# A float32 attention item's product with v turned around, its division moved behind that product, and the first weight decoding kept in source order

## The chip, the core and the metric

The program runs on one NeuronCore of a Trainium2 chip, in one launch. Its engines work side by side, each through its own queue of instructions, in order: TensorE (PE; its weight loads are shown as PEld), VectorE (DVE), ScalarE (ACT), GpSimd (POOL), and SyncE (SP), which only issues DMAs. The metric is the device time of one execution in microseconds. The kernel before takes 966.29 us (median of three runs, 964.24 to 967.59).

## The reference

Causal attention with a window of 128 positions and a slope per head, then two MLPs one behind the other, all in float32:

```python
scores = scale * np.matmul(q, k.transpose(0, 1, 3, 2))            # B=4, H=8, S=576, D=64
scores = np.where(mask, scores + bias[None], -1000000000.0)       # mask: 0 <= rel < 128
attn = np.exp(scores - np.max(scores, axis=-1, keepdims=True))
attn = attn / (np.sum(attn, axis=-1, keepdims=True) + 1e-09)
x = np.matmul(attn, v).transpose(0, 2, 1, 3).reshape(2304, 512)
h = x @ w_in                                                      # 512 -> 2048
x = (np.maximum(h, 0.0) + alpha * np.minimum(h, 0.0)) @ w_out     # 2048 -> 512
h = x @ w_in2
out = (h * (1.0 / (1.0 + np.exp(-1.702 * h)))) @ w_out2
```

The weights arrive as float64.

## The kernel before

**Attention.** An item is one batch, one head and one part of the sequence: part 0 has 256 queries, part 1 has 320. The 64 items come in the order part 0 (batch by batch, head by head), then part 1. The first 16 (`n < FP`) are computed in plain float32, the others by products of high and low halves. For a float32 item, TensorE makes the scores (`a_qk`: tile `s`), VectorE adds the bias and finds the row's extreme value (`a_bias`: tile `tt`, the extreme in `st`), ScalarE takes the exponential and sums it along each row in the same pass (`a_exp`), VectorE turns the sums into reciprocals (`a_recip`), and `a_norm` multiplies each row by its reciprocal: 128 columns on VectorE, 256 on ScalarE. TensorE then transposes the result in three 128x128 pieces (`a_trans`: tile `pt` in PSUM), ScalarE copies them to SBUF (`a_pt_hi`), and `a_av` multiplies: `vz`, padded with zeros to 128 columns so that the two heads of a pair land in the two halves of one PSUM tile `x`, is the stationary operand, and `pt` is streamed, 256 and 128 columns. After the second head of a pair `a_x3` splits `x` into `xh` (ScalarE) and `xl` (VectorE), the input of the first MLP.

**Weights.** Each of the 32 chunks of the first MLP (`w_load`: 512 KB into one of four buffers `ws`) is decoded from float64: two scalings on ScalarE (`w_scale`), then on VectorE `w_sign`, `w_shift` and `w_add`; `w_split` copies the high half `wh` (ScalarE, for two chunks VectorE) and subtracts to get the low half `wl` (VectorE). A buffer is loaded anew after its `w_add`.

**Order.** Rounds `n` = 0 to 9 stand ahead of the first MLP, each with the stages of several items and two decoding steps. Then come the MLP's steps `(k, f)`: `k` is a block of 256 tokens, `f` one of 16 slices of the hidden layer. `m1_h` makes the slice's hidden values (tile `h`, 12 matmuls), `m1_n` and `m1_g` the activation, `m1_o` adds the slice's part of the output (12 matmuls, two steps later). Every two steps carry one more item, and the steps of block 0 carry the rest of the decoding. Slice `f` of block 0 needs chunk `2f` for `m1_h` and chunk `2f + 1` for `m1_o`; block 0 needs items 0 to 7, block 1 items 8 to 15. The program is written in this order, but a scheduler moves instructions on each engine, except where `pin` (`tc.keep_in_program_order`) holds one at its place; before, nothing ahead of the last block of the first MLP is held. The second MLP follows and is not touched.

Of the kernel before, what the change touches and what calls it, by code (L numbers as in the profile page):

```python
# [21 lines left out]
P = 128  # L22
# [43 lines left out]
def tile_window_attention__then__two_mlps(  # L66
# [83 lines left out]
    def w_sign(i):  # L150
        lo, hi = w_words(i)
        pin(nc.vector.tensor_scalar(hi, hi, -0x80000000, None, op0=ALU.bitwise_and))
# [115 lines left out]
    vzs = [apf.tile([P, 2, P], F32, name=f"vz{i}") for i in range(2)]  # L268
# [54 lines left out]
    @stage  # L323
    def a_split_v(n, b, u, h, U):
        nv = (2, 4)[u]
        vr = raw_of(n)[:, UCOLS[u] - nv * D : UCOLS[u]].rearrange("p (j d) -> p j d", d=D)
        if n < FP:
            d0 = (h % 2) * D
            nc.gpsimd.tensor_copy(vzs[n % 2][:, :, d0 : d0 + D], vr)
            return  # L330
        vp = ar["v", n % 2]
        nc.scalar.copy(vp[:, :nv, :D], vr)
        sub("pool", vp[:, :nv, D:], vr, vp[:, :nv, :D])
# [40 lines left out]
    @stage  # L374
    def a_exp(n, b, u, h, U):
        tt, s = tts[n % 2], sts[n % 2]
        for i, (c0, rows, kk, keys) in enumerate(U["chunks"]):
            t = tt[:rows, i * 256 : i * 256 + keys]
            nc.scalar.activation(
                t, t, AF.Exp, bias=s[:rows, i : i + 1], scale=-1.0, accum_out=s[:rows, 4 + i : 5 + i]  # L380
            )

    @stage
    def a_recip(n, b, u, h, U):
        s = sts[n % 2]
        m = len(U["chunks"])
        nc.vector.tensor_scalar(s[:, 8 : 8 + m], s[:, 4 : 4 + m], 1e-9, None, op0=ALU.add)
        nc.vector.reciprocal(s[:, 12 : 12 + m], s[:, 8 : 8 + m])  # L388

    @stage  # L390
    def a_norm(n, b, u, h, U, eng):
        tt, s = tts[n % 2], sts[n % 2]
        for i, (c0, rows, kk, keys) in enumerate(U["chunks"]):
# [34 lines left out]
    def a_av(n, b, u, h, U):  # L428
        if n < FP:
            x = st["x", n] = st["x", n - 1] if h % 2 else ps_a.tile([P, 512], F32, tag="a", name="x")  # L430
            pt, vz = pts[n % 2], vzs[n % 2]
            for j in range(2):
                nc.tensor.matmul(  # L433
                    x[:, j * P : 256], vz[:, j, :], pt[:, j * 256 : 256 + j * P],
                    start=(h % 2 == 0 and j == 0), stop=(h % 2 == 1 and j == 1), skip_group_check=True,
                )
            return
# [12 lines left out]
        st["x", n] = x  # L450

# [17 lines left out]
    def a_x3(n, b, u, h, U):  # L469
# [3 lines left out]
        if n < FP:  # L473
            xp = st["x", n]
# [232 lines left out]
    for t in vzs:  # L707
        nc.gpsimd.memset(t, 0.0)
# [24 lines left out]
    nc.gpsimd.tensor_scalar(beta, alph, -1.0, 1.0, op0=ALU.mult, op1=ALU.add)  # L733
    for n in range(H + 2):

        a_av(n - 2)
# [5 lines left out]
        if n + 1 < H + 2:  # L742
            a_qk(n + 1)
        a_bias(n)
# [3 lines left out]
        a_recip(n - 1)  # L748
        w("shift")
        a_norm(n - 1, "mix")  # L750
        a_trans(n - 1)
        w("add")
        w_ahead()
        w("scale")
        a_x3(n - 2)
        w("split")
        w("sign")
        w("shift")
        a_pt_hi(n - 1, 0)
        a_pt_hi(n - 1, 1)  # L760
        if n + 2 < H + 2:
            a_split(n + 2)
        w("add")
        w_ahead()
        w("scale")
    n = H + 2
    a_split(n)
    for i in range(2):
        a_pt_lo(n - 2, i)
    a_recip(n - 1)  # L770
    a_norm(n - 1, "mix")
    a_av(n - 2)
    a_x1(n - 2)
    a_x2(n - 2)
    a_x3(n - 2)
# [5 lines left out]
    for s, (k, f) in enumerate(steps):  # L781
        n = H + 2 + s // 2
        norm = "mix" if k == 0 else "dve"
        if (k, f) == (KM, 0):
            pinned.append(True)
# [26 lines left out]
        else:  # L812
            a_av(m)
            if n == FP:
# [15 lines left out]
        if k == 0:  # L830
            w("split")
        m1_o(k - (f < LAG), (f - LAG) % NF)
# [131 lines left out]
```

## Time and profile before

| | |
|---|---|
| median of three runs | 966.29 us |
| the profiled execution | 967.92 us |
| its span (first to last instruction) | 966.1 us |
| busy: PE, DVE, ACT, POOL | 97%, 75%, 56%, 9% of the span |
| first instruction on VectorE that computes | 5.38 us |
| `xl` of heads 6 and 7 of batch 0 starts (block 0 can begin in full) | 59.24 us |
| `xl` of heads 6 and 7 of batch 1 starts (block 1 can begin in full) | 125.49 us |

All times in the rows are microseconds from the start of the span. An instruction's duration includes its latency; where two follow each other without a wait, the distance of their starts is the share of the engine's time that one takes.

### The profile page before, as it was taken

How to read it: one execution, taken by the hardware profiler on the slowest of the kernel's cores; microseconds unless marked ns; L12 is line 12 of the kernel's file. 1: busy time of each engine (PE TensorE's matmuls, PEld its weight loads, DVE VectorE, ACT ScalarE, POOL GpSimd, SP SyncE). 2: the span in 40 equal slices, each digit the busy share in tenths (PEclk: the TensorE clock that was granted, in tenths of full speed). 3: DMA queues.
4: the chain of work that ended last, by engine and by line, in shares of the span. 5: the costliest groups of instructions: out<-in, count | busy, mean ns of one | idle time of the engine just before them, and what ended most of it. 6: DMA issues, size and time to landing. Idle time of an engine off the chain costs nothing.

```text
span 966.1 us, 17886 instructions
## 1 busy us (share of the span) xinstructions
PE 939.6 (97%) x6536; PEld 871.2 (90%) x6536; DVE 721.6 (75%) x1789; ACT 536.4 (56%) x1343; POOL 89.8 (9%) x127
## 2 busy tenths in 40 slices
PE   5899999999999999999999999999999999999997
PEld 3579889999999999999988888888898889999997
DVE  6998967767888888887666864697233798878876
ACT  6987766666767667676534443564232644333433
POOL 1000021122222222222000000000000000000000
PEclk9999999999999999999999999999999999999999
DMA  8654521222222223212022335566432333443323
GB/s 266 187 185 148 184 79 56 78 72 66 89 67 88 67 66 89 67 66 89 1 69 81 124 112 182 186 219 200 155 113 88 140 140 114 142 142 113 132 85 109
DMA packets 43895, 112.44 MB, mean 116 GB/s; under 512 B 5024, under 2 KB 15008, under 8 KB 43808
## 3 DMA queue, kind: packets, MB, share of 16 engines
q1 hardware_dynamic: 43808, 111.31, 35.3%
q8 instruction: 51, 0.84, 0.3%
q14 instruction: 36, 0.29, 0.1%
HBM read 82.98 MB, written 28.31 MB: 115 GB/s over the span
## 4 chain that ended last, share of the span: by engine, by line
PE 92%; DMA 3%; ACT 2%; DVE 1%; issue 1%; SPq 0%; DVEq 0%; ACTq 0%
PE h L494 21%; PE h L592 20%; PE p L659 17%; PE o L545 17%; PE p L545 5%; PE x L445 3%; PE pt L412 3%; DMA ws<-in_w_out_dram 2%; PE s L352 1%; PE s L353 1%; PE s L343 1%; PE x L433 1%; ACT ws L148 1%; DMA ws<-in_w_in_dram 0%; ACT oh L102 0%
## 5 line engine op out<-in xcount | busy, mean ns | idle before, releaser
L494 PE MATMUL h<-xh,wh 128*128 128x256 f32 (+1 forms) x512 | 153.7, 302 | 1.0 <-ACT xh L480 0.7
L494 PE MATMUL h<-xh,wl 128*128 128x256 f32 (+1 forms) x512 | 153.6, 300 | 0.0
L494 PE MATMUL h<-xl,wh 128*128 128x256 f32 (+1 forms) x512 | 153.5, 300 | 0.1
L659 PE MATMUL p<-wh,oh 128*128 128x256 f32 x504 | 136.2, 284 | 1.0 <-ACT oh L102 0.6
L659 PE MATMUL p<-wl,oh 128*128 128x256 f32 x504 | 136.1, 283 | 0.0
L545 PE MATMUL o<-gh,wl 128*128 128x256 f32 x448 | 127.5, 286 | 0.0
L545 PE MATMUL o<-gh,wh 128*128 128x256 f32 x448 | 125.4, 286 | 0.0
L545 PE MATMUL o<-gl,wh 128*128 128x256 f32 x448 | 125.2, 281 | 0.0
L659 PE MATMUL p<-wh,ol 128*128 128x256 f32 x504 | 119.2, 284 | 1.0 <-DVE ol L107 1.0
L592 PE MATMUL h<-x2h,wh 128*128 128x512 f32 (+1 forms) x320 | 117.8, 368 | 0.0
L592 PE MATMUL h<-x2l,wh 128*128 128x512 f32 (+1 forms) x320 | 117.7, 368 | 0.0
L592 PE MATMUL h<-x2h,wl 128*128 128x512 f32 (+1 forms) x320 | 117.7, 368 | 0.0
L606 DVE TENSOR_TENSOR g<-h,sg 128x512 f32<-128x512 f32 (+1 forms) x80 | 51.0, 637 | 79.6 <-ACT sg L602 79.5
L602 ACT ACTIVATE sg<-h 128x512 f32<-128x512 f32 (+1 forms) x80 | 44.5, 556 | 107.2 <-PE h L592 106.9
L494 PEld LDWEIGHTS h<-xh,wh 128*128 128x128 f32 x512 | 97.9, 192 | 6.7 <-ACT xh L480 1.9
L494 PEld LDWEIGHTS h<-xl,wh 128*128 128x128 f32 x512 | 98.5, 192 | 5.0 <-DVE st L388 1.3
L494 PEld LDWEIGHTS h<-xh,wl 128*128 128x128 f32 x512 | 98.3, 192 | 2.9
L659 PEld LDWEIGHTS p<-wh,oh 128*128 128x128 f32 x504 | 96.4, 192 | 2.1 <-ACT oh L102 2.0
L659 PEld LDWEIGHTS p<-wl,oh 128*128 128x128 f32 x504 | 96.7, 192 | 0.1
L519 DVE SCALAR_TENSOR_TENSOR g<-n,beta,h 128x256 f32<-128x256 f32 x112 | 53.2, 476 | 46.6 <-ACT n L509 46.4
L659 PEld LDWEIGHTS p<-wh,ol 128*128 128x128 f32 x504 | 86.3, 192 | 1.7 <-DVE ol L107 1.6
L509 ACT ACTIVATE n<-h 128x256 f32<-128x256 f32 x112 | 42.8, 384 | 79.9 <-PE h L494 79.5
(107 smaller groups left out, 2270.7 us busy)
## 6 DMA issues: line engine op xcount, KB each, us to landing
ws<-in_w_in_dram SPq DMA_DIRECT2D x32, 512.0 KB, 3.6
ws<-in_w_out_dram SPq DMA_DIRECT2D x32, 512.0 KB, 3.9
raw<-in_u_dram SPq DMA_DIRECT2D x32, 512.0 KB, 3.4
g2d<-g SPq DMA_DIRECT2D x32, 512.0 KB, 3.4
gr<-g2d SPq DMA_DIRECT2D x32, 512.0 KB, 3.2
raw<-in_u_dram SPq DMA_DIRECT2D x16, 320.0 KB, 2.8
wd<-x2d SPq DMA_DIRECT2D x36, 128.0 KB, 3.0
out_dram<-ob SPq DMA_DIRECT2D x16, 256.0 KB, 3.9
```

The lines of the kernel that those rows point to most:

```text
L148: pin(nc.scalar.mul(lo, lo.bitcast(U32), 2.0**-29))
L343: nc.tensor.matmul(o[:, :keys], raw[:, c0 : c0 + rows], raw[:, 256 + kk : 256 + kk + keys], start=True, stop=True)
L412: nc.tensor.transpose(banks[bank][:, dst : dst + P], src, ident)
L445: nc.tensor.matmul(x[:, oc : oc + nq], v, p[:, col : col + nq], start=(i == 0 and k == 0), stop=(i == len(js) - 1 and k == 1), skip_group_ ...
L494: nc.tensor.matmul(ph, w[:, 0, c * P : (c + 1) * P], x[:, c, r : r + n], start=(c == 0 and i == 0), stop=(c == NC - 1 and i == 2),)
L509: nc.scalar.activation(n, ph, AF.Relu, scale=-1.0)
L519: nc.vector.scalar_tensor_tensor(g, n, beta[:, f : f + 1], ph, op0=ALU.mult, op1=ALU.add)
L545: nc.tensor.matmul(o, w[:, 1, c * P : (c + 1) * P], g, start=(f == 0 and (k == KM or c % 2 == 0) and i == 0), stop=(f == NF - 1 and i == 2 ...
L592: nc.tensor.matmul(ph[:, :n], w[:, f % 2, c * P : (c + 1) * P], x[:, c, :n], start=(c == 0 and i == 0), stop=(c == NC - 1 and i == 2),)
L602: nc.scalar.activation(sg[:, :n], ph[:, :n], AF.Sigmoid, scale=1.702)
L606: nc.vector.tensor_tensor(g[:, f % 2, :n], ph[:, :n], sg[:, :n], op=ALU.mult)
L659: nc.tensor.matmul(o[:, m, :], g[:, a, m * P : (m + 1) * P], w, start=(p == 0 and m == 0 and i == 0), stop=(p == NF // 2 - 1 and i == 2), ...
```

## The change

A float32 item is no longer normalised ahead of its product with v. The exponential is taken without the sum. In `a_av` the transposed exponentials `pt` become the stationary operand, and `vz`, now the 64 columns of v and a column of ones, is streamed: three matmuls of 65 columns, so that the 65th column of the result is the row's sum. The result has queries as rows; for a pair of heads it lies in the PSUM tile `xq`. The new stage `a_div` runs once for a pair: it adds 1e-9 to the four columns of sums, takes reciprocals, and writes the product as an SBUF tile `xq`. `a_x3` then transposes that in two 128x128 pieces into a PSUM tile `x`.

In the rounds ahead of the MLP an item's product now stands in the round of its transposes (it was one round later), the rounds hold 18 decoding steps where they held 20, and all decoding instructions there are held in source order. In the steps of block 0 every fourth step has one decoding step more.

```diff
 def w_sign(i):
     lo, hi = w_words(i)
-        pin(nc.vector.tensor_scalar(hi, hi, -0x80000000, None, op0=ALU.bitwise_and))
+        sign = nc.vector.tensor_scalar(hi, hi, -0x80000000, None, op0=ALU.bitwise_and)
+        if pinned or i < 2 * NF:
+            tc.keep_in_program_order(sign)
...
-    vzs = [apf.tile([P, 2, P], F32, name=f"vz{i}") for i in range(2)]
+    vzs = [apf.tile([P, 2, D + 1], F32, name=f"vz{i}") for i in range(2)]
+    xq = apf.tile([P, 2, 2, D], F32, name="xq")
...
     def a_exp(n, b, u, h, U):
+            if n < FP:
+                nc.scalar.activation(t, t, AF.Exp, bias=s[:rows, i : i + 1], scale=-1.0)
+                continue
...
     def a_av(n, b, u, h, U):
-            for j in range(2):
+            for c, j, col in ((0, 0, 0), (1, 0, 128), (1, 1, 256)):
                 nc.tensor.matmul(
-                    x[:, j * P : 256], vz[:, j, :], pt[:, j * 256 : 256 + j * P],
-                    start=(h % 2 == 0 and j == 0), stop=(h % 2 == 1 and j == 1), skip_group_check=True,
+                    x[:, c, h % 2, :], pt[:, col : col + P], vz[:, j, :],
+                    start=(c == j == h % 2 == 0), stop=(c == j), skip_group_check=True,
                 )
...
+    def a_div(n, b, u, h, U):
+        if n >= FP or h % 2 == 0:
+            return
+        s, x = sts[n % 2], st["xq", n]
+        r, f = (s[:, i : i + 4].rearrange("p (c h) -> p c h", c=2) for i in (8, 12))
+        nc.vector.tensor_scalar(r, x[:, :, :, D], 1e-9, None, op0=ALU.add)
+        nc.vector.reciprocal(f, r)
+        nc.vector.tensor_tensor(xq, x[:, :, :, :D], f.unsqueeze(3).to_broadcast([P, 2, 2, D]), op=ALU.mult)
...
         if n < FP:
-            xp = st["x", n]
+            xp = ps_a.tile([P, 512], F32, tag="a", name="x")
+            for i in range(2):
+                nc.tensor.transpose(xp[:, i * P : (i + 1) * P], xq[:, i, :, :], ident)
...
-        nc.gpsimd.memset(t, 0.0)
+        nc.gpsimd.memset(t, 1.0)
...
+    pinned.append(True)
     for n in range(H + 2):
-        a_av(n - 2)
+        a_trans(n - 1)
         a_split_v(n)
...
+        a_pt_hi(n - 1, 0)
         a_bias(n)
         w("split")
         w("sign")
         a_exp(n)
-        a_recip(n - 1)
+        a_av(n - 1)
         w("shift")
-        a_norm(n - 1, "mix")
-        a_trans(n - 1)
         w("add")
+        a_div(n - 1)
         w_ahead()
         w("scale")
-        a_x3(n - 2)
-        w("split")
-        w("sign")
-        w("shift")
...
+        both = n % 5 < 4
+        if both:
+            w("split")
+            w("sign")
+        a_x3(n - 1)
+        if both:
+            w("shift")
+            w("add")
+            w_ahead()
+            w("scale")
...
+        if (k, f) == (0, 0):
+            pinned.clear()
...
             a_av(m)
+            a_div(m)
...
         if k == 0:
             w("split")
+            if f % 4 == 3:
+                w_decode(lim)
+                w("split")
```

The order of the queues differs only in about the first 1,150 instructions of TensorE, the first 440 of VectorE and the first 325 of ScalarE, which is up to the first steps of block 1; behind that the rows of all engines are the same as before.

VectorE in the rounds ahead of the MLP, around the `xl` of heads 4 and 5 of batch 0 (`wl` are the low halves of weights, `wd` and `ws` a chunk in decoding, `st` the sums and reciprocals), before:

```order
L157 SCALAR_TENSOR_TENSOR wd<-wd,ws 128x512
L107 TENSOR_TENSOR wl_447<-wd,wh_446 128x512
L388 RECIPROCAL st_149<-st_149 128x2
L107 TENSOR_TENSOR xl<-x,xh 128x256
L107 TENSOR_TENSOR wl_488<-wd,wh_487 128x512
L162 ISA wd<-ws,wd 128x1024
L399 TENSOR_SCALAR tt_147<-tt_147,st_149 128x128
L387 TENSOR_SCALAR st_148<-st_148 128x2
L152 TENSOR_SCALAR ws<-ws 128x512
L388 RECIPROCAL st_148<-st_148 128x2
```

In the changed kernel, there around the `xl` of heads 6 and 7 of batch 0:

```order
L107 TENSOR_TENSOR wl_458<-wd,wh_457 128x512
L152 TENSOR_SCALAR ws<-ws 128x512
L465 TENSOR_SCALAR st_149<-xq 128x4
L159 SCALAR_TENSOR_TENSOR wd<-wd,ws 128x512
L466 RECIPROCAL st_149<-st_149 128x4
L164 ISA wd<-ws,wd 128x1024
L467 TENSOR_TENSOR xq<-xq,st_149 128x256
L107 TENSOR_TENSOR wl_502<-wd,wh_501 128x512
L152 TENSOR_SCALAR ws<-ws 128x512
L159 SCALAR_TENSOR_TENSOR wd<-wd,ws 128x512
L107 TENSOR_TENSOR xl<-x,xh 128x256
```

The reciprocals and the multiplication of each item are gone, three instructions for a pair have come, and the same slice of weights (the sixth, with its last low half `wl_447` or `wl_458`) that stood beside the pair 4 and 5 stands beside the pair 6 and 7.

TensorE at the end of block 0, where the product of item 15 (`x` or `xq`) is made, before:

```order
L412 MATMUL pt<-ident,tt_147 128x128
L352 MATMUL s<-kh,q 128x192
L353 MATMUL s<-kl,q 128x192
L352 MATMUL s<-kh,q 128x256
L353 MATMUL s<-kl,q 128x256
L412 MATMUL pt<-ident,tt_147 128x128 x2
L433 MATMUL x<-pt_161,vz_159 128x256
L433 MATMUL x<-pt_161,vz_159 128x128
L494 MATMUL h<-xh,wh_226 128x256
L494 MATMUL h<-xh,wh_270 128x256
```

In the changed kernel (`wh_1197` is a slice of block 0, `o` its output):

```order
L419 MATMUL pt<-ident,tt_147 128x128
L354 MATMUL s<-kh,q 128x192
L355 MATMUL s<-kl,q 128x192
L354 MATMUL s<-kh,q 128x256
L355 MATMUL s<-kl,q 128x256
L419 MATMUL pt<-ident,tt_147 128x128 x2
L513 MATMUL h<-xh,wh_1197 128x256
L513 MATMUL h<-xl,wh_1197 128x256
L440 MATMUL xq<-vz_159,pt_162 128x65 x3
L564 MATMUL o_732<-gh,wh_1080 128x256
L564 MATMUL o_733<-gh,wh_1080 128x256
```

Before, the product stands directly between its transposes and the matmuls that need its `xh` (heads 6 and 7 for slices 0 and 1 of block 1, whose other parts stand ahead of it). In the change 35 matmuls of `h` and `o` stand between the product and the transposes of `xq`, and more behind those, ahead of the first matmul that reads the result.

## Rows read from the trace of the kernel before

**Rows 1.** The page: busy time by engine; PE's busy tenths in 40 slices.

```profile
PE 939.6 (97%) x6536; PEld 871.2 (90%) x6536; DVE 721.6 (75%) x1789; ACT 536.4 (56%) x1343; POOL 89.8 (9%) x127
...
PE   5899999999999999999999999999999999999997
```

**Rows 2.** Stretches: PE, PEld, DVE, ACT, POOL busy (instructions), PEclk, DMA share, GB/s.

```profile
60.00:70.00 10.00, 9.94 (x49) 8.51 (x49) 9.49 (x26) 9.07 (x24) 0.30 (x1) 1.00 0.49 143
...
80.00:100.00 20.00, 20.00 (x164) 19.39 (x163) 18.08 (x46) 15.83 (x37) 0.81 (x2) 1.00 0.53 171
100.00:125.00 25.00, 23.22 (x171) 20.71 (x170) 20.36 (x58) 18.89 (x52) 2.61 (x6) 1.00 0.54 177
125.00:150.00 25.00, 24.35 (x193) 23.95 (x194) 18.46 (x62) 16.80 (x56) 5.70 (x11) 0.93 0.21 68
```

**Rows 3.** Timeline of VectorE: start, length, what; two low halves.

```profile
59.24 0.42 DVE L107 TENSOR_TENSOR xl<-x,xh 128x256 fp32r<-128x256 f32 x1
...
125.49 0.42 DVE L107 TENSOR_TENSOR xl<-x,xh 128x256 fp32r<-128x256 f32 x1
```

**Rows 4.** Timeline of VectorE in the rounds ahead of the MLP, back to back.

```profile
49.30 0.16 DVE L388 RECIPROCAL st<-st 128x2 f32<-128x2 f32 x1
49.38 0.40 DVE L107 TENSOR_TENSOR xl<-x,xh 128x256 fp32r<-128x256 f32 x1
49.70 0.68 DVE L107 TENSOR_TENSOR wl<-wd,wh 128x512 fp32r<-128x512 f32 x1
50.30 0.69 DVE L162 CUSTOM_DVE_ANT_0 wd<-ws,wd 128x1024 uint16<-128x1024 uint16 x1
50.90 0.32 DVE L399 TENSOR_SCALAR tt<-tt,st 128x128 f32<-128x128 f32 x1
...
51.54 0.16 DVE L388 RECIPROCAL st<-st 128x2 f32<-128x2 f32 x1
51.66 0.69 DVE L157 SCALAR_TENSOR_TENSOR wd<-wd,ws 128x512 int32<-128x512 int32 x1
52.27 0.42 DVE L152 TENSOR_SCALAR ws<-ws 128x512 int32<-128x512 int32 x1
52.61 0.28 DVE L399 TENSOR_SCALAR tt<-tt,st 128x128 f32<-128x128 f32 x1
52.80 0.68 DVE L162 CUSTOM_DVE_ANT_0 wd<-ws,wd 128x1024 uint16<-128x1024 uint16 x1
```

**Rows 5.** Groups of ScalarE, 0 to 66 us: busy, mean ns, idle before.

```profile
L397 ACT ACTIVATE tt<-tt,st 128x256 f32<-128x256 f32 x10 | 5.0, 500 | 0.0
...
L379 ACT ACTIVATION_READ_ACCUMULATOR tt<-tt,st 128x1 f32 x20 | 4.0, 198 | 0.0
```

**Rows 6.** Waits, 0 to 66 us: who waited for whom, in total, times, longest.

```profile
DVE ws L152 <- ACT wd L147: 2.1, 3, 1.0
```

**Rows 7.** Timeline of PE at four places: start, length, what, idle before.

```profile
63.75 0.41 PE L494 MATMUL h<-xl,wh 128*128 128x256 f32 x1
63.96 0.41 PE L494 MATMUL h<-xh,wl 128*128 128x256 f32 x1
...
67.83 0.28 PE L494 MATMUL h<-xh,wh 128*128 128x256 f32 x1
67.95 0.28 PE L494 MATMUL h<-xl,wh 128*128 128x256 f32 x1
...
123.88 0.92 PE L433 MATMUL x<-pt,vz 128*128 128x256 f32 x4 [0.88 <-ACT pt L419]
125.51 0.74 PE L494 MATMUL h<-xh,wh 128*128 128x256 f32 x2 [0.71 <-ACT xh L480]
```

**Rows 8.** Chain that ended last, in order of time: start, length, what.

```profile
89.56 0.33 PE pt L412 x3
...
93.42 0.65 PE x L433 x4
```

More of the change, by code (lines that the diff above doesn't have):

```diff
@@ L327, in a_split_v @@
         if n < FP:
-            d0 = (h % 2) * D
-            nc.gpsimd.tensor_copy(vzs[n % 2][:, :, d0 : d0 + D], vr)
+            nc.gpsimd.tensor_copy(vzs[n % 2][:, :, :D], vr)
             return
@@ L386, in a_recip @@
         m = len(U["chunks"])
+        if n < FP:
+            return
         nc.vector.tensor_scalar(s[:, 8 : 8 + m], s[:, 4 : 4 + m], 1e-9, None, op0=ALU.add)
@@ L392, in a_norm @@
         tt, s = tts[n % 2], sts[n % 2]
-        for i, (c0, rows, kk, keys) in enumerate(U["chunks"]):
+        for i, (c0, rows, kk, keys) in enumerate(U["chunks"] if n >= FP else ()):
             t = tt[:rows, i * 256 : i * 256 + keys]
@@ L429, in a_av @@
         if n < FP:
-            x = st["x", n] = st["x", n - 1] if h % 2 else ps_a.tile([P, 512], F32, tag="a", name="x")
+            x = st["xq", n] = st["xq", n - 1] if h % 2 else ps_a.tile([P, 2, 2, D + 1], F32, tag="a", name="xq")
             pt, vz = pts[n % 2], vzs[n % 2]
-            for j in range(2):
+            for c, j, col in ((0, 0, 0), (1, 0, 128), (1, 1, 256)):
                 nc.tensor.matmul(
-                    x[:, j * P : 256], vz[:, j, :], pt[:, j * 256 : 256 + j * P],
-                    start=(h % 2 == 0 and j == 0), stop=(h % 2 == 1 and j == 1), skip_group_check=True,
+                    x[:, c, h % 2, :], pt[:, col : col + P], vz[:, j, :],
+                    start=(c == j == h % 2 == 0), stop=(c == j), skip_group_check=True,
                 )
@@ L450, in a_av @@
         st["x", n] = x
+    @stage
+    def a_div(n, b, u, h, U):
+        if n >= FP or h % 2 == 0:
+            return
+        s, x = sts[n % 2], st["xq", n]
[3 more added lines that the diff above has]
+        nc.vector.tensor_tensor(xq, x[:, :, :, :D], f.unsqueeze(3).to_broadcast([P, 2, 2, D]), op=ALU.mult)
     @stage
@@ L747, in tile_window_attention__then__two_mlps @@
         a_exp(n)
-        a_recip(n - 1)
+        a_av(n - 1)
         w("shift")
-        a_norm(n - 1, "mix")
-        a_trans(n - 1)
         w("add")
+        a_div(n - 1)
         w_ahead()
         w("scale")
-        a_x3(n - 2)
-        w("split")
-        w("sign")
-        w("shift")
[L759 to L765, printed above, removed]
-    n = H + 2
[L767 to L775, printed above, removed]
+        both = n % 5 < 4
[8 more added lines that the diff above has]
+            w("scale")
+    n = H + 2
     at0.close()
```

## Prediction

> **What bounds the kernel now.** I read the page first, for its busy shares and its row of tenths, then the stretches of the first 150 us, the timelines of VectorE and TensorE there, the groups and waits of the same time, and the chain. The reader is to see two regimes. From the third slice of the span on, TensorE's tenths stand at 9 almost to the end [rows 1]; what is taken off another engine there is worth nothing. Ahead of that TensorE is at 5 and 8 tenths, and the work on the first 16 items and the 32 weight chunks sets the pace. Two landmarks divide this part: the low half `xl` of the fourth head pair starts at 59.24 us and lets block 0 begin in full, that of the eighth pair starts at 125.49 and lets block 1 begin [rows 3]. Ahead of the first, VectorE's queue runs mostly back to back [rows 4], and TensorE works at the lower of its clock's two levels: a matmul of 256 columns starts 0.21 us after the one before it at 63.8 us, 0.12 us at 67.8 [rows 7]. (The 1.00 in the stretches can't be relied on there.) Between the landmarks TensorE is full for most of the time, and VectorE has room: busy 9.49 of 10, 18.08 of 20 and 20.36 of 25 us, so 7.1 us idle in 55 [rows 2]. At the second landmark TensorE waits 0.88 us for ScalarE's copy of a transpose, 0.71 us for `xh` [rows 7], and its granted clock falls: 0.93 on average from 125 to 150 us [rows 2], which at half speed is 3.5 us long and costs 1.75 us.
>
> The queues behind the first steps of block 1 are unchanged, and TensorE bounds there. So I expect the end to move by as much as block 1's opening moves.
>
> **The part ahead of block 0.** I count VectorE's queue up to the fourth `xl`, before and changed, by the order of instructions. Signs 17 and 14, shifts 17 and 14, adds 16 and 13, low halves of weights 15 and 13, small operations on sums and reciprocals 19 and 8, normalising multiplications 9 and 0, products that write `xq` 0 and 4; 20 bias instructions, 2 high halves and 4 `xl` in both. Prices are distances of starts in [rows 4]: sign 0.34 (52.27 to 52.61), shift 0.61, add 0.60, low half 0.60, small operation 0.08 (49.30 to 49.38), normalising 0.19 (52.61 to 52.80). The product that writes `xq` has no row: it reads PSUM and has 256 columns, like `xl`, 0.32; bounds are 0.19 (a 128-column multiplication) and 0.60 (512 columns), which for four is -0.5 to +1.1 us; I take 0.32. The denominators read four columns of PSUM: 0.08 as the others, at most 0.2, which for four is +0.5. The sum is 3 x 0.34 + 3 x 0.61 + 3 x 0.60 + 2 x 0.60 + 11 x 0.08 + 9 x 0.19 - 4 x 0.32 = 1.02 + 1.83 + 1.80 + 1.20 + 0.88 + 1.71 - 1.28 = 7.2 us less ahead of the landmark.
>
> ScalarE loses more than that for an item, the multiplication over 256 columns and two reads of the accumulator, busy 5.0 and 4.0 us for ten items [rows 5], and gets nothing in return. So it does not take VectorE's place. The weights' transfers do not either: three chunks fewer must have landed by the landmark.
>
> The pinned decoding and the division add waits: VectorE stands at the denominators until TensorE has made the pair's product, and behind them in the queue stand a shift, an add and the next `wl`, for which `w_scale`, the next load and slice of `h` wait. Before, the scheduler could put something else there; VectorE waited for ScalarE's scaling three times, 2.1 us in all [rows 6]. Bounds: nine rounds with one such wait each, 0.7 us on average, cost 6.3 us; at the other end the old 2.1 us go. I take no change: in the queue the denominators stand about four VectorE instructions of a round behind the exponentials on which the product waits.
>
> **TensorE in the items.** The product had two matmuls with 384 streamed columns, four records, 0.65 us for an item at the high clock [rows 8]; it gets three matmuls of 65 columns, six records, each with its own load of 128-column weights. Nearest rows: three transposes, each with 128-column float32 weights of its own, take 0.33 in the same group, 0.11 each. Six at that price are 0.66; by streamed columns alone it is 0.65 x 195/384 = 0.33. The pair's two new transposes add 0.22, so 0.11 for an item. An item thus goes from 0.65 to between 0.44 and 0.77; seven or so items between the landmarks give -1.5 to +0.8 us. I take 0, near the dearer end, since the transposes are the nearer row. Ahead of the first landmark all this counts double, at the low clock, +1.9 us at the worst for eight items, and lies beside VectorE's queue.
>
> The Trainium skill speaks here, in "TensorE: Matmul & The Clock Gate", section "LDWEIGHTS (loading the stationary operand)": a weight load costs by its columns, P/1.2 ns, however little is streamed behind it. Six loads of 128 columns would be an estimated 0.64 us by that page, no less than now, and the two transposes come on top: some 0.7 us slower over seven items, where counting columns gives 1.5 us faster. The trace's 0.11 for a transpose agrees with such a load but can't tell it from its streaming.
>
> **Between the landmarks.** VectorE gets what was put off: 3 signs, 3 shifts, 3 adds and 1 low half more, 4 products, against 5 small operations and 7 normalisings less: 1.02 + 1.83 + 1.80 + 0.60 + 1.28 - 0.40 - 1.33 = 4.8 us. Its cover is the 7.1 idle us named above; without cover it is 4.8 us late. At the end, the product of item 15 no longer stands directly ahead of the matmuls that need its `xh`: 35 matmuls stand behind it. So I count the waits of 0.88 and 0.71 us as gone, 1.6 us. The fall of the clock behind them, 1.75 us, I leave out of the sum: other waits can bring it, with VectorE this full.
>
> The sum is 7.2 + 1.6 = 8.8 us. The profiled execution took 967.92 us, of which 966.1 is span; it would take 959.1. It lies 1.6 us above the median of the runs shown, so for the median 966.3 - 8.8 = 957.5 us.
>
> **The rivals.** (1) VectorE becomes the bound of block 0, and the put-off decoding comes back in full: 7.2 - 4.8 = 2.4 us remain, 963.9 us. For it: 90% busy from 80 to 100 us already [rows 2], and late slices need their chunk just as it is decoded. Against: items also lose work, and ScalarE gets freer.
>
> (2) Slower. In block 0 TensorE, faster than the decoding, stands before undecoded slices, as it stands now before items at 124 and 125.5 us [rows 7], and the clock falls each time. One such event costs 1.6 us of waiting and 1.75 of low clock, 3.4 us [rows 2, 7]. From rival 1's 2.4 us left, the second event decides between faster and slower; with three the time is 966.3 - 2.4 + 10.2 = 974 us. Against: a TensorE at the low clock needs twice as long for a slice, so VectorE catches up, and one event is rather the number than three.
>
> (3) The start does not move: the waits of the pinned queue take 6.3 of the 7.2 us. With the 1.6 us of the end, 963.8 us; without them 965.4. For it: nothing can pass a waiting instruction among the decoding. Against: three decodings fewer stand ahead of the landmark, wherever the waits are.
>
> (4) More than forecast: the old waits of the start (2.1), the clock's fall (1.75) and cheaper products (1.5) all go: 8.8 + 5.4 = 14.2 us, 952.1 us.
>
> **How the numbers follow.** I give the forecast 0.64, its own range 954 to 962 us; rival 1 0.13, rival 2 0.07, rival 3 0.10, rival 4 0.06. About 0.3% either way (963.4 to 969.2) is what a measurement of this kernel can tell from no change. The forecast and rival 4 are faster, and with a third or so of rivals 1 and 3, which straddle the edge: 0.78. The rest of these two is no change, 0.15; slower is rival 2, 0.07. The range runs from 951.5, rival 4's end, to 965.5, which takes in rivals 1 and 3.
>
> **What would show it.** The fourth pair's `xl` should start near 52 us, the eighth's at about 116 or earlier; later than 57 for the first says rival 3. VectorE busy above 95% from there to block 1, with TensorE idle for `wl` or `wh`, says rival 1; a granted clock below 1.00 there more than once says rival 2. The three matmuls of a product at the high clock should take 0.33 to 0.66 us. TensorE's busy time from 200 us on should not change; if the end moves by more or less than block 1's opening, my reading that TensorE alone bounds the rest is wrong.

## The result, and the profile after

The changed kernel takes 971.74 us (median of seven runs, 969.37 to 975.83); the kernel before, in seven runs beside them, 965.71 (963.68 to 967.59). The ratio is 1.0069, 95% interval 1.0046 to 1.0093: slower by 0.7%, where 957.5 us was forecast and 965.5 was the end of the range. The profiled execution after took 971.74 us (span 970.0), 3.8 us more than that of before. From 195 us on, the landmarks of the trace stand a constant 3.2 us later (3.9 at the end). TensorE is never idle from 150 to 600 us in either trace, so only the first 160 us are looked at below. The medians lie 6.0 us apart; where the 2.2 us that these two traces don't show come from stays open.

The page of after, its busy line and PE's tenths, against [rows 1]. TensorE's and VectorE's totals hardly differ; the first slices do, 4 and 8 where 5 and 8 stood:

```profile
PE 940.0 (97%) x6584; PEld 875.6 (90%) x6584; DVE 720.3 (74%) x1765; ACT 528.1 (54%) x1295; POOL 89.4 (9%) x127
...
PE   4889899999999999999999999999999999999997
```

The two low halves of [rows 3] in the timeline of VectorE. The forecast had them near 52 and at about 116:

```profile
59.78 0.42 DVE L107 TENSOR_TENSOR xl<-x,xh 128x256 fp32r<-128x256 f32 x1
...
126.57 0.42 DVE L107 TENSOR_TENSOR xl<-x,xh 128x256 fp32r<-128x256 f32 x1 [0.18 <-ACT xh L499]
```

So the start did not move, although VectorE has less to do ahead of it. The stretch from 0 to 60 us (columns as in [rows 2]; VectorE is the third figure), before and after:

```profile
0.00:60.00 60.00, 43.75 (x124) 29.31 (x125) 48.64 (x142) 47.40 (x114) 7.11 (x24) 1.00 0.73 224
...
0.00:60.00 60.00, 40.74 (x143) 30.29 (x143) 42.23 (x112) 38.02 (x76) 5.36 (x23) 1.00 0.67 199
```

VectorE is busy 42.23 us after, 48.64 before. That is 6.4 us less work, close to the 7.2 that were counted. The work went as counted; the time of it became waiting. VectorE's waits from 8 to 62 us of after (who waited for whom: us in total, times, longest):

```profile
DVE tt L365 <- PE s L345: 5.5, 5, 1.8
DVE wl L107 <- ACT wh L102: 2.8, 6, 0.7
DVE tt L365 <- DMA raw<-in_u_dram: 2.1, 1, 2.1
DVE ws L152 <- ACT wd L147: 1.9, 1, 1.9
```

and of before, where beside the 2.1 us of [rows 6] only this stood:

```profile
DVE tt L363 <- PE pt L412: 1.2, 3, 0.7
DVE st L387 <- ACT tt L379: 0.5, 1, 0.5
DVE tt L363 <- PE s L343: 0.4, 1, 0.4
DVE wl L107 <- ACT wh L102: 0.3, 1, 0.3
```

Together that is 12.3 us against 4.5. The largest new wait is VectorE's bias for TensorE's scores. What TensorE does then is seen in one round trip. First VectorE, in the timeline, against the back-to-back queue of [rows 4]:

```profile
31.47 0.29 DVE L365 CUSTOM_DVE_ANT_0 tt<-s,relht 128x128 f32<-128x128 f32 x1 [1.16 <-PE s L345]
...
32.03 0.69 DVE L107 TENSOR_TENSOR wl<-wd,wh 128x512 fp32r<-128x512 f32 x1
32.64 0.42 DVE L152 TENSOR_SCALAR ws<-ws 128x512 int32<-128x512 int32 x1
32.97 0.15 DVE L465 TENSOR_SCALAR st<-xq 128x4 f32<-128x4 f32 x1
33.09 0.77 DVE L159 SCALAR_TENSOR_TENSOR wd<-wd,ws 128x512 int32<-128x512 int32 x1
33.79 0.16 DVE L466 RECIPROCAL st<-st 128x4 f32<-128x4 f32 x1
33.90 0.69 DVE L164 CUSTOM_DVE_ANT_0 wd<-ws,wd 128x1024 uint16<-128x1024 uint16 x1
34.51 0.42 DVE L467 TENSOR_TENSOR xq<-xq,st 128x256 f32<-128x256 f32 x1
```

and TensorE beside it, in the same time:

```profile
31.64 1.27 PE L440 MATMUL xq<-vz,pt 128*128 128x65 f32 x5
34.98 0.69 PE L493 MATMUL x<-ident,xq 128*128 128x128 f32 x2 [2.07 <-DVE xq L467]
35.46 0.84 PE L419 MATMUL pt<-ident,tt 128*128 128x128 f32 x3
36.24 1.65 PE L345 MATMUL s<-rawf 64*128 64x128 f32 x4
...
42.78 1.54 PE L440 MATMUL xq<-vz,pt 128*128 128x65 f32 x6
46.39 0.69 PE L493 MATMUL x<-ident,xq 128*128 128x128 f32 x2 [2.07 <-DVE xq L467]
```

TensorE ends the pair's product at 32.9 and stands 2.07 us before the transposes of `xq`, because a shift and an add of about 0.7 us each stand between the three instructions of the division. Behind the transposes in its queue stand the next item's transposes and scores, so the scores are late, and VectorE in turn stands before its bias. The same wait comes once for each of the four pairs, in TensorE's waits up to 62 us:

```profile
PE x L493 <- DVE xq L467: 8.9, 4, 2.7
```

From 34.98 to 44.32 us TensorE works without a break, 9.3 us at the low clock (its 256-column matmuls start 0.21 us apart there), and then it stands 2.07 us. These two make up the 11.4 us that lie between two pairs' `xl` in this trace. The first pair's `xl` starts 3.0 us earlier than before (24.80, 27.79 before), and the next three give that up.

The stretches of [rows 2] after (columns as there):

```profile
60.00:70.00 10.00, 10.00 (x46) 8.80 (x46) 8.02 (x21) 7.99 (x19) 0.42 (x2) 1.00 0.50 144
80.00:100.00 20.00, 20.00 (x163) 19.01 (x163) 18.14 (x47) 15.25 (x36) 2.00 (x2) 1.00 0.56 173
100.00:125.00 25.00, 22.10 (x156) 19.87 (x156) 23.83 (x62) 19.86 (x46) 2.62 (x3) 0.93 0.54 165
125.00:150.00 25.00, 25.00 (x215) 25.00 (x215) 18.76 (x61) 17.56 (x57) 5.62 (x11) 1.00 0.37 125
```

From 100 to 125 us VectorE is at 95% (20.36 us before, 23.83 now) and TensorE has 2.9 us idle. Its timeline there names what it waits for; the waits for the end of items that stood at 124 and 125.5 us [rows 7] are gone, and these have come:

```profile
110.54 0.39 PE L513 MATMUL h<-xh,wh 128*128 128x256 f32 x1 [1.48 <-ACT wh L102]
...
117.86 0.38 PE L513 MATMUL h<-xh,wh 128*128 128x256 f32 x1 [0.83 <-ACT wh L102]
...
118.85 0.88 PE L440 MATMUL xq<-vz,pt 128*128 128x65 f32 x6 [0.49 <-ACT pt L426]
```

14 chunks are through `w_add` when block 0's first `g` starts, 17 before; the last of the 32 low halves starts at 127.9 us, at 117.1 before. The account by TensorE's idle time: to 60 us 19.3 (16.2 before), from 100 to 125 us 2.9 (1.8), from 125 to 150 us 0 (0.65). That is 3.4 us more, against a shift of 3.2. It is an account of idle time alone: the pitch of the 256-column matmuls also falls from 0.21 to 0.12 us later, at about 69 us after and 67.6 before.

The product itself, at the high clock, against [rows 8] (0.65 us for an item):

```profile
78.10 0.78 PE L440 MATMUL xq<-vz,pt 128*128 128x65 f32 x6
78.69 0.36 PE L513 MATMUL h<-xl,wh 128*128 128x256 f32 x1
...
93.30 0.38 PE L493 MATMUL x<-ident,xq 128*128 128x128 f32 x2
93.52 0.49 PE L419 MATMUL pt<-ident,tt 128*128 128x128 f32 x3
```

From 78.10 to 78.69 is 0.59 us for an item, and the pair's transposes take 0.22. With half of these an item comes to 0.70, inside the 0.44 to 0.77 of the prediction.

### The profile page after: what moved, and what is told of

The parts are those of the page before. It is cut to its first block, busy times and chain, and to the rows that moved or that the text cites. A ratio compares the mean times of both kernels' runs of the same rounds, so it can differ in the third digit from the quotient of the medians.

```text
span 970.0 us, 17871 instructions
## 1 busy us (share of the span) xinstructions
PE 940.0 (97%) x6584; PEld 875.6 (90%) x6584; DVE 720.3 (74%) x1765; ACT 528.1 (54%) x1295; POOL 89.4 (9%) x127
## 4 chain that ended last, share of the span: by engine, by line
PE 88%; DVE 5%; DMA 3%; ACT 2%; issue 1%; SPq 0%; DVEq 0%; ACTq 0%
PE h L611 20%; PE h L513 20%; PE p L678 17%; PE o L564 15%; PE p L564 5%; PE x L452 3%; PE pt L419 3%; DMA ws<-in_w_in_dram 2%; PE s L354 1%; PE s L355 1%; PE s L345 1%; DMA rawf<-in_u_dram 1%; DVE wl L107 1%; DVE wd L159 1%; DVE wd L164 1%
```

## The experiments

The theory that the first reading gave: the division sends VectorE's result back into TensorE's in-order queue within one round, and both engines pay for the round trip (A in the texts below). Its rivals: the decoding that is put off to block 0, or the new order of the rounds and the hold, loses by itself (B, D). From e13 on a second part joins it: items that run ahead of held decoding (C). Each text says what its letters stand for; in those of e4 to e8, C is that VectorE's decoding decides, and in that of e3, D is that the turned product is dear in itself.

Ratios are against the kernel before on the same chip, with 95% intervals. Measured beside the times, for each kernel: when block 0's first `g` starts and how many chunks are through `w_add` by then, when the last low half of the first MLP starts, and TensorE's idle time from 0 to 160 us (160 less its busy time in that stretch).

| kernel | first g, us | adds by then | last low half, us | PE idle, us | ratio |
|---|---|---|---|---|---|
| before | 62.0 | 17 | 117.1 | 18.7 | 1 |
| after | 62.5 | 14 | 127.9 | 22.2 | 1.0069 |
| e1 | 52.3 | 10 | 136.7 | 25.6 | 1.0149 [1.0118, 1.0180] |
| e2 | 69.4 | 20 | 113.5 | 25.9 | 1.0074 [1.0055, 1.0093] |
| e3 | 75.1 | 22 | 110.8 | 29.5 | 1.0096 [1.0077, 1.0115] |
| e4 | 50.6 | 8 | 154.0 | 34.4 | 1.0243 [1.0216, 1.0270] |
| e5 | 59.7 | 14 | 123.7 | 22.5 | 1.0035 [1.0022, 1.0048] |
| e6 | 62.1 | 14 | 129.2 | 25.8 | 1.0074 [1.0053, 1.0095] |
| e7 | 61.0 | 11 | 146.3 | 31.2 | 1.0205 [1.0174, 1.0236] |
| e8 | 62.2 | 17 | 118.0 | 19.0 | 1.0001 [0.9985, 1.0017] |
| e9 | 72.7 | 15 | 133.4 | 31.5 | 1.0132 [1.0106, 1.0157] |
| e10 | 77.4 | 16 | 137.4 | 36.2 | 1.0152 [1.0126, 1.0179] |
| e11 | 48.0 | 8 | 143.5 | 34.2 | 1.0150 [1.0122, 1.0179] |
| e12 | 49.5 | 9 | 143.3 | 31.9 | 1.0141 [1.0115, 1.0167] |
| e13 | 65.7 | 17 | 118.7 | 18.9 | 0.9990 [0.9980, 1.0000] |
| e14 | 66.9 | 19 | 117.5 | 23.1 | 1.0020 [1.0006, 1.0035] |
| e15 | 58.7 | 14 | 123.7 | 22.2 | 1.0029 [1.0014, 1.0044] |
| e16 | 62.0 | 16 | 121.5 | 22.9 | 1.0040 [1.0025, 1.0055] |
| e17 | 69.9 | 16 | 127.8 | 25.3 | 1.0075 [1.0058, 1.0092] |
| e18 | 66.8 | 17 | 120.9 | 20.0 | 1.0006 [0.9993, 1.0019] |

Over the table the loss goes with TensorE's idle time. For all but e1, e4 and e7, which lose some 7 us more, a kernel's extra time lies within about 3 us of its extra idle time. That is a pattern, not a test.

### The parts of the change apart: e2, e3

`e2_no_pin` is the change without the hold; `e3_turned_alone` is the turned product and its division in the rounds of before, with 20 steps and no hold (`a_div` stands ahead of `a_x3(n - 2)`).

```diff
-    pinned.append(True)
     for n in range(H + 2):
...
-        sign = nc.vector.tensor_scalar(hi, hi, -0x80000000, None, op0=ALU.bitwise_and)
-        if pinned or i < 2 * NF:
-            tc.keep_in_program_order(sign)
+        pin(nc.vector.tensor_scalar(hi, hi, -0x80000000, None, op0=ALU.bitwise_and))
```

> Edit: no instruction of the decoding ahead of the last block of the first MLP is held in source order; all else as in the change. Theory A (round trip): TensorE's queue still has the transposes of xq directly behind the pair's product and ahead of the next item's transposes and scores, so its waits for VectorE remain at 1.5 to 2.5 us per pair; time within 3 us of the change, 969 to 975 us. Theory B (pinned order): VectorE's queue can bring the division forward and the rest closes up; waits of TensorE under 0.5 us per pair, time 960 to 966 us.

> Edit: the product with v turned and divided by a column of sums as in the change, but the rounds, the 20 decoding steps and the free order as in the kernel before (product one round behind its transposes, division and transposes of xq directly behind it in the source). Theory A (round trip): the turned product itself costs TensorE nothing, what costs is where the transposes of xq stand; here the product of the next item stands behind them, the next transposes partly ahead, so waits of about 1 us per pair, time 963 to 969 us. Theory D (the turned product is dear on TensorE at the low clock): the fourth xl starts at 62 us or later, time 970 us or more.

973.46 and 975.19 us. e2 came out in A's range, with longer waits than A said; e3 missed A's range and lies in D's, whose reason e13 takes away below. The turned product alone, in e3, costs 9 us. VectorE has done more here than in the change (45 to 47 us busy by 60 us, against 42), yet block 0 opens 7 to 13 us late: the scheduler spreads the division among the decoding, and TensorE stands before `xq`. VectorE's three instructions for the fourth pair in e2, in its timeline:

```profile
61.16 0.15 DVE L463 TENSOR_SCALAR st<-xq 128x4 f32<-128x4 f32 x1
...
62.17 0.16 DVE L464 RECIPROCAL st<-st 128x4 f32<-128x4 f32 x1
...
63.77 0.42 DVE L465 TENSOR_TENSOR xq<-xq,st 128x256 f32<-128x256 f32 x1
```

and TensorE's transposes behind them:

```profile
64.25 0.69 PE L491 MATMUL x<-ident,xq 128*128 128x128 f32 x2 [4.32 <-DVE xq L465]
```

So the round trip is there with and without the hold; with the hold TensorE waits less (2.08 for 4.32 at the fourth pair) and VectorE more for TensorE's scores (5.5 for 1.1 us from 8 to 62 us).

### The wait taken away under the hold: e1, e4, e7

e1 moves `a_x3` by a round. e4 lets the transposes read the identity, so that TensorE never waits for the division (it leaves the attention of these items out of the result). e7 is e1 with 20 decoding steps and an extra step of decoding in every step of block 0.

```diff
-        a_x3(n - 1)
+        a_x3(n - 2)                # e1, e7: behind a_qk(n + 1)
...
-                nc.tensor.transpose(xp[:, i * P : (i + 1) * P], xq[:, i, :, :], ident)
+                nc.tensor.transpose(xp[:, i * P : (i + 1) * P], ident, ident)   # e4
```

> Edit: in the rounds ahead of the MLP the transposes of xq and the split into xh and xl are written one round later, behind the next scores (pair n-2 instead of n-1); all else as in the change. Theory A (round trip): in the change TensorE stands 2.1 to 2.7 us per pair, 8.9 us in four pairs, at the transposes of xq until VectorE has divided, and the next item's transposes and scores, for which VectorE then waits 10.8 us in all, stand behind them in its queue. With other work of TensorE in between, these waits fall under 0.5 us per pair, the period of a pair falls from 11.4 to about 9.3 us, and although the fourth pair comes a round later its xl starts at 55 to 58 us instead of 59.8; time 962 to 968 us, at or under before. Theory B (pinned order): the waits move elsewhere, the period stays near 11 us, time 970 to 975 us.

> Edit: the two transposes of a pair read the identity instead of xq, so that they do not wait for VectorE; the division is still done and its product is written, but the values that enter the first MLP are those of the identity. Theory A (round trip): the 8.9 us of TensorE's waits ahead of block 0 go, the fourth xl starts at 51 to 53 us, and block 0 ends by as much earlier less 3 to 4 us of VectorE's put-off decoding; time 961 to 966 us. Theory C (VectorE bounds block 0 however early it opens): the fourth xl comes as early, but VectorE is full to block 1's opening, TensorE waits for weights, and the time stays at 968 to 972 us. Theory B (pinned order): the fourth xl moves by under 2 us.

> Edit: as e1 (transposes of xq written one round later), with two decoding steps in all ten rounds and two in every step of block 0. e1 had its fourth xl at 48.4 us, a pair every 6.6 to 8.2 us instead of 11.4, but only 10 chunks decoded then, and its last low half came at 136.7 us. Theory C: what e1 lacked was decoding, not time of TensorE; with more of it in the queue the last low half comes at 112 to 122 us and the time is 960 to 968 us, under e1's 982 by 14 us or more. Theory B (the held order is what starves the decoding): the last low half stays beyond 128 us, time 972 us or more.

982.37, 989.29 and 988.07 us: e1 and e4 lie above the ranges of all their theories, e7 in B's. The wait is gone in e4 and halved in e1 and e7 (4.3 us by 60 us, two of the four pairs still at about 2 us). The landmark came earlier, `xl` of the fourth pair at 48.4, 47.7 and 55.1 us (59.78 in the change), and the time went the other way. Block 0 opens with 8 to 11 chunks decoded. TensorE then stands before weights and before what VectorE and ScalarE owe the next items, at a lower granted clock (0.80 to 0.93 in the stretches from 100 to 150 us), beside a VectorE that is 95 to 98% busy from 100 to 125 us. In e4:

```profile
100.00:125.00 25.00, 16.28 (x103) 14.13 (x101) 24.01 (x61) 21.70 (x57) 3.68 (x6) 0.92 0.55 177
```

The wait was thus not the whole cause under the hold.

### Where the decoding steps stand: e5, e6, e8

e5 is the change with 20 steps in the rounds, e6 with an extra step in every step of block 0, e8 the kernel before with 18 steps and the extra ones.

```diff
-        both = n % 5 < 4
+        both = True                # e5
...
-            if f % 4 == 3:
+            if True:               # e6
```

> Edit: all ten rounds ahead of the MLP hold two decoding steps (20 in all, as in the kernel before) instead of 18; all else as in the change. Theory C (VectorE's total to the last decoded chunk decides, and its idle time ahead of block 0 is what was lost): in the change VectorE has been busy 44.4 us when block 0's first slice leaves it at 62.5 us, 51.1 in the kernel before. If two more decodings fill idle time there, the fourth xl comes at most 1 us later, the last low half of the first MLP's weights 3 to 4 us earlier than the change's 127.9, and the time falls by 2 to 4 us to 967 to 970. Theory A (round trip alone, TensorE's waits per pair): the two steps lengthen two rounds by their 2.1 us each, the fourth xl comes 2 to 4 us later, time as the change or up to 2 us more.

> Edit: in block 0 every step has the extra decoding step (two chunks a step until all are decoded) instead of every fourth; all else as in the change. Theory C: from 60 to 100 us VectorE is 80 to 95% busy because its queue follows TensorE's steps; with two chunks a step it fills, the last low half comes at 115 to 122 us instead of 127.9, TensorE no longer waits for weights, time 965 to 969 us. Theory A: block 0 is late only by its opening; nothing moves by more than 1.5 us, or slices wait longer behind decoding, time 970 to 974 us.

> Edit: the kernel before, with the product as it was and nothing held, but with 18 decoding steps in the rounds and the extra one in every fourth step of block 0, as the change has them. Theory C: putting off two decodings (about 2.1 us of VectorE each) costs their full length where VectorE has no idle time left in block 0, and nothing where it has: in the kernel before it idles 7 us of 55, so the time is within 3 us of before, 964 to 969 us, well under the change. If the put-off alone makes the loss, the time is 970 us or more.

971.18, 974.45 and 967.69 us (before beside them: 967.67). Putting off two decodings costs nothing by itself (e8). With the division there, more decoding ahead gains some by the ratios (e5; its interval and that of the change just touch, and 971.18 us lies above C's range and in A's), and more of it in block 0 nothing (e6, a miss for C: the last low half comes at 129.2 us, not at 115 to 122).

### The division in one piece, under the hold: e9, e10

```diff
-        nc.vector.tensor_scalar(r, x[:, :, :, D], 1e-9, None, op0=ALU.add)
+        pin(nc.vector.tensor_scalar(r, x[:, :, :, D], 1e-9, None, op0=ALU.add))   # and the other two
...
+        a_div(n - 1)
         w("shift")
         w("add")
-        a_div(n - 1)
```

> The changed kernel with the three instructions of the division held directly behind one another and ahead of the round's shift and add, which before stood between them. Theory A (VectorE starves on the round trip from TensorE's product through the division back to TensorE's transposes of xq): TensorE's wait for xq falls from 2.07 us a pair to about 0.9, the pairs' period from 11.4 to about 10.2 us, VectorE has 44 to 46 us of work done by 60 us (42.2 in the changed kernel), and the time is 966 to 969 us. Theory B (the round trip is no cause of the loss): the waits get shorter, and the time stays at 970 to 974 us.

> The same as e9_div_together with 20 decoding steps in the rounds where the change has 18 (the later extra steps then find nothing left to do). Theory A: the shorter wait and the longer queue of decoding add up, 963 to 968 us. Theory B: no better than the changed kernel with 20 steps alone (971.2 us), at least 970.

979.03 and 980.98 us: a miss in e9, and in e10 B's number. Held, the division keeps its place behind all decoding that stands ahead of it in the source, and the end of one decoding and the whole of another come first. In e9 the product is done at about 32 us, the denominators start at 38.62, and TensorE's timeline shows

```profile
39.50 0.69 PE L493 MATMUL x<-ident,xq 128*128 128x128 f32 x2 [7.36 <-DVE xq L467]
```

The edit lengthened the wait that it was to shorten, and the time rose with it.

### The hold without the division: e11, e12

e11 is the old product in the changed rounds with hold, 18 steps and extra steps; e12 the kernel before with the hold alone.

```diff
+    pinned.append(True)
     for n in range(H + 2):
...
+        if (k, f) == (0, 0):
+            pinned.clear()
```

> The old product (rows normalised ahead of the transposes, v padded as the stationary operand, no division behind) in the changed rounds: their new order of stages, the decoding held in source order, 18 steps and the later extra ones. Theory A (the division puts VectorE between two pieces of TensorE's work in one round): without it there is no such wait, VectorE has at least 47 us of work done by 60 us, and the time is 963 to 968 us. Theory B (the new order of the rounds, or the held decoding, loses by itself): 969 to 973 us, and VectorE has no more than 44 us done by 60 us.

> The kernel before, with nothing changed but that the first decoding is held in source order in the rounds ahead of the first MLP. Theory A: with no division among the decoding the held order costs little, VectorE has at least 47 us done by 60 us, and the time is within 2 us of the kernel before (964 to 968 us). Theory B: holding the order is itself what starves VectorE, 969 to 974 us, at most 44 us done by 60 us.

980.81 and 980.26 us. Here my theory fell and its rival did not go far enough: with no division at all, the hold costs 13 us. It holds the decoding only among itself; the items' instructions are free, and the scheduler lets them run ahead. Nine chunks are decoded when block 0 opens, and they are fewer at the same time too (9 adds by 50 us, 13 before). The stretches of e12 show the bill, TensorE 6.6 and 6.4 us idle at a lower granted clock beside a VectorE at 91% and 96%:

```profile
80.00:100.00 20.00, 13.43 (x70) 11.61 (x70) 18.11 (x49) 17.07 (x46) 3.71 (x8) 0.83 0.54 176
100.00:125.00 25.00, 18.59 (x115) 16.92 (x116) 24.02 (x61) 20.75 (x50) 4.63 (x5) 0.86 0.54 170
```

### The wait taken away with nothing held: e13, e15

e13 is e3 with the transposes a round later, e15 is e3 with the identity as in e4 (it leaves the same attention out).

```diff
         a_div(n - 2)
-        a_x3(n - 2)
+        a_x3(n - 3)
...
     n = H + 2
+    a_x3(n - 3)
     a_split(n)
```

> The turned product alone in the rounds of the kernel before, nothing held (e3_turned_alone, 975.2 us, where TensorE waits 11 us for xq ahead of 60 us), with the transposes of xq one round later in the source, so that a whole round of TensorE's work lies between product and transposes. Theory A (the cost of the turned product is TensorE's wait for the division): the waits for xq fall below 2 us in total, block 0 opens about 8 us earlier than in e3_turned_alone (its first g before 69 us), 965 to 969 us. Theory B (its cost lies elsewhere, in the added instructions or in VectorE's queue): at least 973 us.

> The turned product alone (e3_turned_alone, nothing held), with the two transposes reading the identity matrix instead of xq: the attention of the 16 float32 items is left out of the result, all instructions are there, and TensorE never waits for the division. Theory A (that wait is the cost): 964 to 969 us, block 0's first g before 69 us. Theory B: at least 973 us.

966.52 and 969.65 us, beside 967.23 for the kernel before: e13 as expected, e15 a little above its range. In the waits of TensorE up to 70 us, e3 has

```profile
PE x L491 <- DVE xq L465: 14.5, 4, 4.5
```

and e13

```profile
PE x L491 <- DVE xq L465: 1.9, 1, 1.9
```

with the same added instructions. So the cost of the turned product goes with TensorE's wait for the division: from 975.19 to 966.52 us (as ratios, since the chips differ, from 1.0096 to 0.9990). e15 shows that the wait is not all: without any, block 0 opens at 58.7 us with 14 chunks, and TensorE stands 6.6 us from 100 to 125 us, 3.4 of them for ScalarE's `wh`. So items can run ahead of decoding with nothing held. Block 0 of e13 opens at 65.7 us with 17 chunks decoded, and from 80 to 150 us TensorE is never idle:

```profile
80.00:100.00 20.00, 20.00 (x163) 19.00 (x162) 18.77 (x48) 15.82 (x36) 0.87 (x2) 1.00 0.55 175
100.00:125.00 25.00, 25.00 (x209) 24.37 (x209) 21.90 (x60) 18.27 (x50) 3.34 (x7) 1.00 0.47 155
125.00:150.00 25.00, 25.00 (x217) 25.00 (x216) 19.28 (x63) 18.44 (x60) 5.50 (x9) 1.00 0.31 99
```

### The items held too: e16, e17

e16 is e12, e17 is e1, each with VectorE's bias of the rounds held among the decoding.

```diff
-            nc.vector.tensor_tensor_reduce(
+            bias = nc.vector.tensor_tensor_reduce(
...
+            if n < H + 2:
+                pin(bias)
```

> The kernel before with the decoding held (e12_before_pinned, 980.3 us, 9 adds done at the first g of block 0), and VectorE's bias instructions of the rounds held in the same order. Theory C (holding the decoding among itself lets the items' free instructions run ahead of it, so that block 0 opens with too few chunks and TensorE waits for weights): with the items held too, 14 or 15 adds stand ahead of the first g, TensorE's idle time from its first h to 160 us falls from 20 to under 12 us, 966 to 972 us. Theory D (any holding starves VectorE): 978 to 984 us again.

> The changed kernel with both repairs: the transposes of xq one round later (e1_x3_later, 982.4 us, 10 adds done at the first g) and VectorE's bias instructions of the rounds held among the decoding. Theory C with A (the wait for the division is one cost, items that run ahead of the held decoding the other): waits for xq under 2 us, 15 or 16 adds done at the first g, which comes before 61 us, 961 to 967 us. Theory D (any holding starves VectorE): 971 us or more.

e16: 970.68 us, 16 adds by the first `g`, TensorE idle 13.3 us from its first `h` (20.1 in e12, under 12 was expected). Most of the hold's 13 us is gone, so items running ahead is most of its cost. e17: 974.86 us, a miss, and D's number. The waits for `xq` are gone and 16 adds are done, but block 0 opens at 69.9 us; the round trip has moved to the next one in the row. With the bias behind decoding, the exponentials are late, and TensorE waits in its timeline for those:

```profile
63.80 0.48 PE L421 MATMUL pt<-ident,tt 128*128 128x128 f32 x1 [4.27 <-ACT tt L384]
```

VectorE is busy only 38.9 us by 60 us there (42.2 in the change), so this run does not exclude D.

### Two combinations: e14, e18

e14 is e1 without the hold; e18 is e13 with 18 steps and the extra ones of block 0.

> The changed kernel with its transposes of xq one round later in the source and the decoding not held (e1_x3_later without the hold, e2_no_pin with the later transposes). Theory A (the wait for the division is what the turned product costs, and the hold is what lets the items run ahead in e1): the waits for xq ahead of 70 us fall from 14.5 us (e2_no_pin) below 3 us, at least 14 adds are done at the first g, and the time is 964 to 969 us. Theory B (the changed rounds lose by themselves): 971 us or more.

> e13_alone_later (966.5 us), with 18 decoding steps in the rounds instead of 20 and the later extra step of the change. Theory A: the two steps put off find VectorE with room, since the items cost it less, and block 0 opens about 2 us earlier, 962 to 966 us. Theory C (what opens block 0 earlier lets the items run ahead of the decoding): no gain, 966 to 970 us, the granted clock falls again between 100 and 125 us.

e14: 970.21 us, between the two ranges, and a miss for A's waits. In three of the four pairs the transposes now stand behind the next scores in TensorE's queue, in e2 directly behind the product. But nothing holds the division, and VectorE still spreads it among the decoding (for the fourth pair the three instructions start at 55.56, 56.84 and 58.70 us), so the waits up to 70 us hardly fall (14.5 in e2):

```profile
PE x L491 <- DVE xq L465: 11.6, 4, 4.7
```

In e13 the product of the next pair's first item stands between as well.

e18: 968.42 us, no gain, though the clock stays at 1.00 from 100 to 125 us and not even the first `g` comes earlier (66.8). Best of all is e13, level with the kernel before.

## Why the prediction was wrong

**The part ahead of block 0** failed, and with it the sum. "The sum is ... 7.2 us less ahead of the landmark" counted one queue. VectorE's work fell by 6.4 us as counted, and the landmark moved by +0.5 us, because VectorE did not bound that part once the division stood in it. The prediction looked for what could take VectorE's place and weighed ScalarE and the transfers. TensorE's product at the low clock it named, +1.9 us at the worst, and put "beside VectorE's queue". In the trace TensorE's 9.3 us of work for a pair and its wait of 2.07 us for the division fill the 11.4 us between pairs. e4 shows it by experiment: with that wait taken away and all else as in the change, the fourth `xl` starts at 47.7 us for 59.78.

**The waits of the pinned queue** were sized from one side. The bound of nine waits of 0.7 us, 6.3 us, put them on VectorE before the denominators. There VectorE did not wait at all; TensorE waited behind them, four times, 8.9 us, and VectorE for TensorE's scores. 7.8 us more of waiting on VectorE than before is above the bound (2.1 of it comes before the first division, behind a transfer), and "no change" was taken.

**The cover in block 0** was right as a number and wrong as a use: 7.1 us idle were to hide 4.8 us. With the start not moved, block 0 opens with three chunks fewer at the same time, and the last low half comes 10.8 us later than before. This is rival 1 on top of rival 3, whose sign, a fourth `xl` later than 57 us, came. The prediction priced them one at a time (963.9, and 963.8 to 965.4) as if they excluded each other. Its own terms together, 0.9 us gained and 4.8 lost, are an estimated 3.9 us slower, or 2.3 with the 1.6 us at the end. Of rival 2 there is only the beginning: two waits for weights (1.48 and 0.83 us), one fall of the clock (0.93 from 100 to 125 us, in place of that of 125 to 150).

**The waits at the end of block 0** (0.88 and 0.71) went as said; those for weights took their place.

**TensorE in the items** was right: 0.59 us for 0.65, with 0.11 for the transposes. e13 shows it in the time: all added instructions together cost nothing that can be measured. The reading that nothing counts behind block 1 held but for the last 0.7 us: the shift stands at 3.2 us from 195 us to behind 720. The sign that was set for it, an end that moves as block 1's opening does, failed: the eighth `xl` starts 1.1 us later, the end comes 3.9 us later. With no wait at that landmark any more, its start does not measure how much work TensorE still has ahead.

What the runs show as the cause: the division puts VectorE between two pieces of TensorE's work in one round (e3 against e13, some 9 to 10 us). The hold alone costs 13 us in the kernel before (e12), mostly because free items run ahead of held decoding (e16 gives back some 10). In the changed kernel these meet and partly cancel: the waits slow the items down, so that the held decoding keeps up better (14 chunks against 8 to 11 in e1, e4, e11 and e12). That last sentence is how I read the table; no run separates it. Open is also why the two repairs together (e17) are no better than the change, beyond the new wait that its trace shows, and whether the change with the hold has a version that keeps both; none was found in these runs.

## What to carry to other kernels

A step that sends a result from one in-order engine through another and back is paid at the first engine's queue, not by the length of the step: here three instructions of about 0.7 us in all cost TensorE 2.1 us and more a pair, up to 4.5 where nothing is held (e3). Put a full round of other work between sending and using (e13), and count both queues before counting work saved. An edit that makes an early stage shorter gains only if what the next stage needs is also ready; here the five kernels that opened block 0 ahead of 59 us (e1, e4, e11, e12, e15) did so with 8 to 14 chunks decoded, and all lost. Order held for some instructions of a queue and free for the rest lets the rest overtake (e12, e16).

## What was not expected of the hardware

An item's three matmuls of 65 columns, in the trace six records with a load of 128 columns each, cost about as much as 384 streamed columns. The six records of an item's product start 0.11 us apart at the high clock (0.59 us in all, the first two closer) and 0.21 apart at the low one. By the old product's pace (384 columns in 0.65 us, [rows 8]) the 195 columns would take 0.33 us. The Trainium skill, "TensorE: Matmul & The Clock Gate", section "LDWEIGHTS (loading the stationary operand)", has a load cost P/1.2 ns, with P its columns; by that an estimated 0.107 us for each, and the trace at the high clock agrees with its 0.11. The transposes at 93.30 us, with 128 columns streamed, also take 0.11 each, so it is not the streamed columns that set the pace here.
